# Z of batch 0 loaded in parts while its rows are made, in an FFT, channel mix and MLP kernel

## The chip, the cores and the metric

The kernel runs on one core of a Trainium2 chip. Its time is device microseconds of one launch. A median of several runs stands for a kernel; beside it there is one profiled execution, whose trace gives the rows that are shown here.

## What is computed

The input x has 8 batches of 3136 tokens and 256 channels, in float32. The first part goes through the frequency domain: a real FFT over the tokens, a complex channel mix, a soft threshold, and the inverse FFT. The second part adds a low-rank token mix and a two-layer MLP with a residual.

```python
X = np.fft.rfft(x, axis=1);  Xr, Xi = X.real, X.imag
Yr = Xr @ w_r - Xi @ w_i + b_r;  Yi = Xr @ w_i + Xi @ w_r + b_i
Y = soft(Yr, 0.01) + 1j * soft(Yi, 0.01)      # sign(v) * max(|v| - 0.01, 0)
y = np.fft.irfft(Y, n=3136, axis=1)
h = y.transpose(0, 2, 1) @ U @ V              # U is 3136 x 32, V is 32 x 3136
u = y + h.transpose(0, 2, 1)
out = u + np.maximum(u @ w_ch1, 0.0) @ w_ch2  # 256 -> 1024 -> 256
```

## The kernel before

The FFT of 3136 points is split into 49 x 64. For each batch there are four stages and then the MLP.

- Stage A makes products over the 49 points. Their rows go to the DRAM buffer gd. For batch 0 alone they stay in SBUF, in the tile t0.
- The frequency stage makes, for each pair of the frequencies 1 to 24 and for frequency 0 alone, the 64-point products (b_unit, PSUM psb), the channel mix (mix_unit, psy for batch 0), the soft threshold (rl on ScalarE, ys on VectorE), a split of the result into a high and a low part (yh on ScalarE, yl on GpSimd, which is written y where both stand in one tile), and the first half of the inverse (c_unit, psc). ScalarE evicts the result into a tile zs, and a DMA stores it as rows of the DRAM buffer zd. A pair with first frequency k0 writes the four rows from 2 k0 - 2 on; frequency 0 writes row 48. So zd has 49 rows of 64 tokens of 256 channels, 64 KB to a row.
- Stage D needs all 49 rows, turned: a tile zt holds, for 4 of the 32 token positions i and both halves j, the 49 rows on the partitions from 64 j on. It makes 512 small products of 49 x 64 by 49 x 81 in batch 0, four at a time in quarters of the array, into the PSUM tiles psd. ScalarE evicts them to xq, VectorE sums the part that belongs to U (pa). The right-hand sides du hold constants and U's part, which make_ud makes (psu).
- p_unit (psp, pt) and u_prep (psv) begin the MLP, whose token windows, six for each batch, follow one another. l1_chunks and l2_chunks are the layers (psx, psy, psz; pso), each a fast matrix product in split float32.

From window 0 on, the stages of the next batch run beside the MLP. Before window 0 only batch 0's stages can run, beside the decoding of the 64-bit weights: V, U, w1 and w2 come as words (dw) and are turned to float32 on ScalarE and VectorE, in tiles dm, dl, dp of the tag sv (four buffers). V's two halves go through a tile full of the tag tt (one buffer) to DRAM.

The order of the work has two sources. The function bodies record operations in a program order; for batch 0 a list called first holds units with a position, and is sorted: c_unit of unit q has position 3 q + 5, after_store(q) means 3 q + 5.5, and the units of D have 100, 105 and so on. The decoding is a generator that steps takes forward, a part at a time. Then a planner (class _Program, from line 166 on) sorts all operations by its own costs and due times, for each engine. All loads and stores but a few are issued by SyncE, in one queue; a load is released 16 us (LEAD) ahead of its due time. The buffers of a tag are given out in the order in which the program first touches them. Where the planner expects that TensorE will wait, it puts in matmuls of the identity (line 540, "ident"), as many as the expected gap divided by 0.222 us.

Frequency 0 is the last unit of batch 0 (pairs). Odd units put y and zs in the tag xz (five buffers), which the tiles zt of z use too; the last three zt stand in the tag rl. z_load (line 1085) is called by d_unit in D's place; for each c it issues two loads of 48 rows and one of row 48. Thus a load of z waits for a free buffer of xz or rl and for the stores of its rows. Loads of batch 1's input (xt, a_load, line 714) use the tag xz as well.

These lines say how z is loaded:

```python
pl, tg, n = (fp, "xz", 5) if b or c < 5 else (mp, "rl", 3)
zt = pl.tile([128, 4, D], F32, tag=tg, name=f"zt_{b}_{c}", bufs=n)
nk = KP if b else K1 - 1
loads = [dma.dma_start(zt[64 * j : 64 * j + nk], zv[c, j, 0:nk]) for j in range(2)]
if nk < K1:
    loads.append(dma.dma_start(by_row(zt)[nk], zv[c, :, nk]))
```

Of the kernel before, what the change touches and what calls it, by code (L numbers as in the profile page):

```python
# [13 lines left out]
F32 = mybir.dt.float32  # L14
# [536 lines left out]
def fft_mix_moe_kernel(  # L551
# [159 lines left out]
    def by_row(t):  # L711
        return t.rearrange("(j n) i d -> n j i d", j=2)

    def a_load(b, c):
        xt = fp.tile([128, 4, D], F32, tag="xz", name=f"xt_{b}_{c}", bufs=5)
        nk = KP if b < NB - 1 else K1 - 1
        n0, i = K1 * b, slice(4 * c, 4 * c + 4)
        loads = [dma.dma_start(xt[64 * j : 64 * j + nk], xj[n0 : n0 + nk, j, i]) for j in range(2)]
        if nk < K1:
            loads.append(dma.dma_start(by_row(xt)[nk], xj[n0 + nk, :, i]))  # L720
        a_state[b, c] = xt
        return loads

    def a_mm(b, c, loads=()):
# [51 lines left out]
    def shared(b):  # L776
        return b % 2 == 1 and b + 1 < NB

    def pairs(b):
        p = [(1 + 2 * q, 2) for q in range(12)]  # L780
        if shared(b):
            p.append((0, 2))
        elif b == 0 or b % 2 == 1:
            p.append((0, 1))
        return p

# [40 lines left out]
    def b_early(q):  # L827

        load_t(0, q)
        ts, fbt = s_state[0, q]  # L830
        ps = psm([128, 2, 2, 128], f"psb_0_{q}")
        for k in range(2):
            pe.matmul(ps[:, 0, k, :], lhsT=ts[k][0], rhs=fbt[:, k, :], start=True, stop=True)
        s_state[0, "ps", q] = ps

    def b_mm(b, q):
# [41 lines left out]
    def mix_unit0(q):  # L878
        n = pairs(0)[q][1]
        xx = s_state.pop((0, q, "x"))  # L880
        ps = ps_f.tile([128, 2, D], F32, tag="psf", name=f"psy_{q}")

        pe.matmul(
            ps[:, 0:n].rearrange("p k (n t) -> p k n t", t=2),
            lhsT=first_w["one"],
            rhs=paired(first_w["bias"]).unsqueeze(1).broadcast_to([128, n, D // 2, 2]),
            start=True,
            stop=False,
        )
        for k in range(n):  # L890
            todo = []
            for h in range(2):
                for c, w in ((1, wm[0]), (0, first_w["wi"])):
                    l = [x[:, h, k, c : c + 2].rearrange("p c f -> p (c f)") for x in xx]
                    todo.append((l, [v[:, h, :] for v in w]))
            for j, (l, w) in enumerate(todo):
                mm3(ps[:, k], l, w, False, k == n - 1 and j == len(todo) - 1, False)
        rl = ybuf(0, q, "rl")
        act.activation(rl[:, 0:n], ps[:, 0:n], AF.Relu, bias=lam)
        ys = ybuf(0, q, "ys")  # L900
        dve.scalar_tensor_tensor(
            out=ys[:, 0:n], in0=ps[:, 0:n], scalar=LAM, in1=rl[:, 0:n], op0=ALU.add, op1=ALU.min
        )
        if q % 2:
            both = fp.tile([128, 2, 2, D], F32R, tag="xz", name=f"y_0_{q}", bufs=5)
            yh, yl = both[:, 0], both[:, 1]
        else:
            yh, yl = [fp.tile([128, 2, D], F32R, tag="y" + k, name=f"y{k}_0_{q}", bufs=1) for k in "hl"]
        split(yh[:, 0:n], yl[:, 0:n], ys[:, 0:n], pool)
        s_state[0, q, "y"] = (yh, yl)  # L910

    def b_unit(b, q):
# [82 lines left out]
    def c_unit(b, q):  # L995
        k0, n = pairs(b)[q]
        yy = s_state.pop((b, q, "y"))
        pl, tg = (ps_f, "psf") if b or q % 2 == 0 else (ps_o, "pso1")
        ps = pl.tile([128, 2, D], F32, tag=tg, name=f"psc_{b}_{q}")
        mo = 128 if k0 else 64  # L1000
        mm3(ps[:mo, 0:n], fc if k0 else fc0, [k[:, 0:n] for k in yy], True, True, pairs=b > 0 or n == 2)
        if b == 0 and q % 2:
            zs = fp.tile([128, 2, D], F32, tag="xz", name=f"zs_{b}_{q}", bufs=5)
        else:
            zs = fp.tile([128, 2, D], F32, tag="zs", name=f"zs_{b}_{q}")
        if b == 0:
            zv = zs[:mo, 0:n].rearrange("p k (t n) -> p k t n", t=2)
            acopy(zv, flat(ps[:mo, 0:n]).rearrange("p (n t k) -> p k t n", k=n, t=2))
        elif n == 2:
            acopy(zs[:mo], halves(ps[:mo]))  # L1010
        else:
            acopy(whole2(zs[:mo, 0:1]), halves2(ps[:mo, 0:1]))
        if k0:
            dma.dma_start(rows(zd[b % 2], k0), zs)
        else:
            for k in range(n):
                dma.dma_start(zd[(b + k) % 2][K1 - 1], zs[0:64, k])
# [64 lines left out]
    def pad_z(k):  # L1082
        dma.dma_start(zd[k][K1:KP], x[0, 0 : (KP - K1) * N2].rearrange("(k n) d -> k n d", k=KP - K1))

    def z_load(b, c):

        pl, tg, n = (fp, "xz", 5) if b or c < 5 else (mp, "rl", 3)
        zt = pl.tile([128, 4, D], F32, tag=tg, name=f"zt_{b}_{c}", bufs=n)
        zv = zd[b % 2].rearrange("k (j c i) d -> c j k i d", j=2, i=4)
        s_state[b, "z", c] = zt  # L1090
        nk = KP if b else K1 - 1
        loads = [dma.dma_start(zt[64 * j : 64 * j + nk], zv[c, j, 0:nk]) for j in range(2)]
        if nk < K1:
            loads.append(dma.dma_start(by_row(zt)[nk], zv[c, :, nk]))
        return loads

    def dt_load(b, t):
        n0, n = UNITS_D[t]
# [6 lines left out]
    def d_unit(b, t, du, loads=()):  # L1105
        if t == 0:
            p_state[b] = qp.tile([128, 2, 3, R], F32, tag="pa", name=f"pa_{b}", bufs=1)
        n0, n = UNITS_D[t]
        hf = n0 // NH
        if n0 % NH == 0:  # L1110
            xq[b, hf] = qp.tile([128, 2, NH, NP], F32, tag="xq", name=f"xq_{b}_{hf}", bufs=3)
        if du is None:
            dt_ = s_state.pop((b, "d", t))
        else:
            dt_ = du[t]
            for c in range(8):
                if 4 * c < n0 + n and (b, "z", c) not in s_state:
                    z_load(b, c)
        pa = p_state[b]
        xv_ = xq[b, hf].rearrange("p h i (q j) -> p h j i q", j=2)  # L1120
        i0 = n0 % NH
        for h in range(2):
            turn_d[0] += 1
            ps = banks(turn_d[0] if b == 0 else 0, f"psd_{b}_{t}_{h}")

            def products():
                for k in range(n):
                    at = C81 * k - R * (k % 2)
                    for j in range(2):
                        for e in range(2):  # L1130
                            pe.matmul(
                                ps[j][64 * e : 64 * e + 64, at : at + C81],
                                lhsT=s_state[b, "z", (n0 + k) // 4][
                                    64 * j : 64 * j + K1,
                                    (n0 + k) % 4,
                                    128 * h + 64 * e : 128 * h + 64 * e + 64,
                                ],
                                rhs=dt_[64 * j : 64 * j + K1, C81 * k : C81 * k + C81],
                                start=k == 0,
                                stop=k == n - 1,  # L1140
                                tile_position=(64 * j, 64 * e),
                                skip_group_check=True,
                            )

            first = in_group(products)
            if h == 0:
                first.preds.update((e.n, e) for e in loads)
            for j in range(2):
                p = ps[j][:, 0 : n * C81]
                acopy(xv_[:, h, j, i0 : i0 + n], p.rearrange("p (n c) -> p n c", c=C81)[:, :, 0:K1])  # L1150
                u = p.rearrange("p (q c) -> p q c", c=2 * C81)[:, :, K1:C81]
                if t == 0 and j == 0:
                    dve.tensor_copy(pa[:, h], u)
                else:
                    v = pa[:, h, 0 : n // 2]
                    dve.tensor_tensor(out=v, in0=v, in1=u, op=ALU.add)
# [50 lines left out]
    def load_words(src, shape, name):  # L1207
        pp, *dims = shape
        n = int(_np.prod(dims))
        w = mp.tile([128, 1024], U32, tag="rh", name="dw_%s%d%d" % name, bufs=3)  # L1210
        w = w[:pp, : 2 * n].rearrange("p (n t) -> p n t", t=2)
        dma.dma_start(w if len(dims) == 1 else w.rearrange("p (f d) t -> p f d t", f=dims[0]), src)
        words[name] = w

    def decode(name, hi=None, lo=None, full=None):
# [282 lines left out]
            after_mix(q, 1.5 + k + (q == 0), steps, 1)  # L1498
    after_mix(12, 2.6, steps, STEPS_W)
    on(99.5, wait_2)  # L1500
    for n in range(16):
        on(100.5 + 2 * n, steps, 1)

# [455 lines left out]
```

## Time and profile before

| what | value |
|---|---|
| median of 3 runs | 1606.91 us (1606.64 to 1608.23) |
| profiled execution | 1603.72 us |
| its span | 1601.9 us |
| mean granted clock of TensorE | 0.995 |
| instructions | 37505 |
| VectorE busy | 1268.8 us (79%) |
| ScalarE busy | 937.5 us (59%) |
| GpSimd busy | 433.3 us (27%) |
| DMA | 209.16 MB, mean 131 GB/s |

The span runs from the first to the last instruction of the trace; the profiled execution's own time is 1.8 us longer. PE is TensorE, PEld its weight loads, DVE VectorE, ACT ScalarE, POOL GpSimd, SP SyncE. All operations go through one line of the planner, L542, so a row is told apart by the names of the tiles: psd<-du,zt is a product of stage D. L540 is a filler product. In a timeline a row gives the start, the duration, the operation, and in brackets the idle time of the engine before it with what ended it. In a table of windows the granted clock is 1.00 at full speed and 0.50 at half.

### The profile page before, as it was taken

What the parts mean: (1) busy time and instruction counts of PE and PEld (TensorE: products, weight loads), DVE (VectorE), ACT (ScalarE), POOL (GpSimd) and SP (SyncE); (2) the same over time, 40 slices, a digit from 0 to 9 for tenths busy, and PEclk for the clock granted to TensorE, in tenths of its full rate; (3) what the DMA queues carried; (4) which work ended last, traced back from release to release, by engine and by line L of the source; (5) the groups of instructions that cost most, each with busy time, mean ns of one, the idle gap of its engine ahead of it and who ended that gap; (6) DMA issues with size and microseconds to landing.
All of it is one profiled execution on the core that took longest, in us unless ns stands there. A gap on an engine that the chain in (4) does not pass through costs nothing.

```text
span 1601.9 us, 37505 instructions
## 1 busy us (share of the span) xinstructions
PE 1575.6 (98%) x14528; PEld 1428.1 (89%) x14528; DVE 1268.8 (79%) x2478; ACT 937.5 (59%) x1982; POOL 433.3 (27%) x406
## 2 busy tenths in 40 slices
PE   8988999999999999999999999999999999999998
PEld 6986898999889889999888988989988999989997
DVE  6866889679966898769975888868996789866785
ACT  3855666556655666556655666556665566555543
POOL 1320333123312332223331233314331233312221
PEclk9989999999999999999999999999999999999999
DMA  9776564516664454714574365433756024520332
GB/s 235 207 162 183 152 195 133 153 52 175 181 177 116 127 158 117 177 31 133 154 202 116 112 178 150 117 91 86 180 147 197 28 74 128 130 75 14 81 61 39
DMA packets 224814, 209.16 MB, mean 131 GB/s; under 512 B 127834, under 2 KB 195968, under 8 KB 224588
## 3 DMA queue, kind: packets, MB, share of 16 engines
q1 hardware_dynamic: 221998, 205.90, 48.1%
q8 instruction: 115, 1.88, 0.5%
q10 hardware_dynamic: 2638, 0.86, 0.3%
q14 instruction: 63, 0.52, 0.1%
HBM read 126.59 MB, written 81.81 MB: 130 GB/s over the span
## 4 chain that ended last, share of the span: by engine, by line
PE 89%; DVE 5%; DMA 2%; issue 1%; ACT 1%; SPq 1%; POOL 1%; DVEq 0%; POOLq 0%; ACTq 0%
PE pso L542 31%; PE psy L542 16%; PE psx L542 8%; PE psq L542 7%; PE psd L542 5%; PE psb L542 5%; PE psz L542 4%; PE psa L542 4%; PE psc L542 4%; PE pst L542 3%; PE psv L542 1%; SPq L542 1%; DVE ys L542 1%; DMA zd<-zs 1%; DVE s L542 0%
## 5 line engine op out<-in xcount | busy, mean ns | idle before, releaser
L542 PE MATMUL pso<-rh,w2t 128*128 128x512 f32 x1568 | 405.3, 381 | 0.0
L542 PEld LDWEIGHTS pso<-rh,w2t 128*128 128x128 f32 x1568 | 274.5, 190 | 26.7
L542 PE MATMUL pso<-rl,w2t 128*128 128x512 f32 x784 | 233.4, 379 | 0.0
L542 POOL TENSOR_TENSOR yl<-ys,yh 128x512 fp32r<-128x512 f32 (+1 forms) x95 | 122.5, 1290 | 219.8 <-ACT yh L542 121.2
L542 ACT ACTIVATE rh<-s 128x512 fp32r<-128x512 f32 x196 | 122.2, 628 | 89.6 <-DVE s L542 82.9
L542 DVE SCALAR_TENSOR_TENSOR rl<-s,rh 128x512 fp32r<-128x512 f32 x196 | 149.3, 767 | 25.2 <-ACT rh L542 23.6
L542 DVE SCALAR_TENSOR_TENSOR ys<-tb,rl 64x256 f32<-64x256 f32 x350 | 155.1, 443 | 16.7 <-ACT rl L542 12.0
L542 PEld LDWEIGHTS pso<-rl,w2t 128*128 128x128 f32 x784 | 148.3, 189 | 20.9
L542 POOL TENSOR_TENSOR tl<-ts,th 128x256 fp32r<-128x256 f32 x88 | 66.9, 760 | 300.3 <-DVE ys L542 130.4
L542 PE MATMUL psq<-wmt,xsh 128*128 128x256 f32 (+1 forms) x704 | 123.5, 277 | 0.0
L542 PE MATMUL psy<-odh,w1t 128*128 128x256 f32 x784 | 122.8, 279 | 0.0
L542 PEld LDWEIGHTS psy<-odh,w1t 128*128 128x128 f32 x784 | 109.8, 191 | 10.4 <-issue 2.4
L542 PEld LDWEIGHTS psq<-wmt,xsh 128*128 128x128 f32 (+1 forms) x704 | 109.3, 191 | 2.6 <-ACT xt L542 0.8
L542 POOL TENSOR_TENSOR obl<-xq,obh 128x512 fp32r<-128x512 f32 x47 | 58.7, 1249 | 194.5 <-ACT obh L542 51.4
L542 POOL TENSOR_TENSOR ocl<-xq,och 128x256 fp32r<-128x256 f32 x47 | 34.5, 733 | 244.3 <-DVE tt L542 92.9
L542 ACT ACTIVATE xq<-psd 128x294 f32<-128x294 f32 (+1 forms) x192 | 69.7, 437 | 50.0 <-PE psd L542 48.8
L542 DVE TENSOR_TENSOR v<-v,psy 128x512 f32<-128x512 f32 x98 | 66.7, 680 | 40.1 <-PE psy L542 21.6
L542 PE MATMUL psq<-wmt,xsl 128*128 128x256 f32 (+1 forms) x352 | 96.8, 275 | 0.0
L542 ACT ACTIVATE rh<-v 128x512 fp32r<-128x512 f32 x98 | 61.8, 631 | 59.4 <-DVE v L542 57.2
L542 DVE TENSOR_TENSOR s<-psz,s 128x512 f32<-128x512 f32 x98 | 67.2, 686 | 36.7 <-PE psz L542 27.4
L542 POOL TENSOR_TENSOR odl<-tt,odh 128x512 fp32r<-128x512 f32 x48 | 64.0, 1334 | 112.1 <-ACT odh L542 87.9
L542 PE MATMUL psb<-fb,t 128*128 128x128 f32 (+1 forms) x700 | 92.7, 276 | 0.0
(209 smaller groups left out, 3971.2 us busy)
## 6 DMA issues: line engine op xcount, KB each, us to landing
gd<-xt SPq DMA_DIRECT2D x112, 224.0 KB
zt<-zd SPq DMA_DIRECT2D x112, 224.0 KB
zd<-zs SPq DMA_DIRECT2D x96, 256.0 KB
out_dram<-os SPq DMA_DIRECT2D x190, 128.0 KB
xt<-in_x_dram SPq DMA_DIRECT2D x96, 224.0 KB
t<-gd SPq DMA_DIRECT2D x84, 256.0 KB
fb<-in_fb_dram SPq DMA_DIRECT2D x96, 128.0 KB
vw<-vd SPq DMA_DIRECT2D x44, 256.0 KB
```

Of the source, the lines that this page charges most:

```text
L542: made = call(*[real(a) for a in op.args], **{k: real(a) for k, a in op.kw.items()})
```

## The change

Frequency 0 becomes the first unit of batch 0. The odd units' zs move from the tag xz to the tag tt. The last two units (q 11 and 12) split y on VectorE instead of GpSimd. Stage D of batch 0 no longer calls z_load. Instead z is loaded into four tiles: two of 12 positions each in the tag xq (three buffers, of which fdt, the constants for make_ud, has one), one in the tag os, one in xz. Each tile gets its rows in three parts: rows 0 to 23 and row 48 after the stores of unit 6, rows 24 to 39 after those of unit 10, rows 40 to 47 at position 99.6. The loads of batch 1's input, all but those of the first tile, and the loads of words that come later in the program than the second part, wait for the latest part of z (after_z). Batches 1 to 7 load z as before.

```diff
     def a_load(b, c):
...
+        if b == 1 and c > 0:
+            for e in loads:
+                after_z(e)
...
     def pairs(b):
         p = [(1 + 2 * q, 2) for q in range(12)]
-        if shared(b):
+        if b == 0:
+            p.insert(0, (0, 1))
+        elif shared(b):
             p.append((0, 2))
-        elif b == 0 or b % 2 == 1:
+        elif b % 2 == 1:
             p.append((0, 1))
...
-        for k in range(2):
-            pe.matmul(ps[:, 0, k, :], lhsT=ts[k][0], rhs=fbt[:, k, :], start=True, stop=True)
+        k0, n = pairs(0)[q]
+        kk = 128 if k0 else 64
+        for k in range(n):
+            pe.matmul(ps[:, 0, k, :], lhsT=ts[k][0][:kk], rhs=fbt[:kk, k, :], start=True, stop=True)
...
-        split(yh[:, 0:n], yl[:, 0:n], ys[:, 0:n], pool)
+        split(yh[:, 0:n], yl[:, 0:n], ys[:, 0:n], pool if q < 11 else dve)
...
         if b == 0 and q % 2:
-            zs = fp.tile([128, 2, D], F32, tag="xz", name=f"zs_{b}_{q}", bufs=5)
+            zs = mp.tile([128, 2, D], F32, tag="tt", name=f"zs_{b}_{q}")
...
+    Z_CUT = (0, 24, 40, K1 - 1)
+    z_parts = ((0, 3), (3, 3), (6, 1), (7, 1))
+
+    def z_range(c, n, j, k0, k1):
+        zt = s_state[0, "zp", c]
+        src = zd[0][k0:k1, 32 * j + 4 * c : 32 * j + 4 * c + 4 * n]
+        return dma.dma_start(zt[64 * j + k0 : 64 * j + k1], src)
+
+    def z_early(m):
+        c, n = z_parts[m]
+        if n == 3:
+            zt = qp.tile([128, 12, D], F32, tag="xq", name=f"zx_{c}", bufs=3)
+        elif c == 6:
+            zt = mp.tile([128, 4, D], F32, tag="os", name="zt_0_6")
+        else:
+            zt = fp.tile([128, 4, D], F32, tag="xz", name="zt_0_7", bufs=5)
...
+        for j in range(2):
+            z_range(c, n, j, *Z_CUT[0:2])
+            z_range(c, n, j, K1 - 1, K1)
+
+    z_end = []
+
+    def z_late(m, part):
+        c, n = z_parts[m]
+        z_end[:] = [z_range(c, n, j, *Z_CUT[part : part + 2]) for j in range(2)]
+
+    def after_z(load):
+        load.preds.update((e.n, e) for e in z_end)
+        return load
...
-            for c in range(8):
-                if 4 * c < n0 + n and (b, "z", c) not in s_state:
-                    z_load(b, c)
...
-        dma.dma_start(w if len(dims) == 1 else w.rearrange("p (f d) t -> p f d t", f=dims[0]), src)
+        after_z(dma.dma_start(w if len(dims) == 1 else w.rearrange("p (f d) t -> p f d t", f=dims[0]), src))
...
+    for m in range(4):
+        after_store(6 + m / 2, z_early, m)
+        after_store(10 + m / 2, z_late, m, 1)
+        on(99.6, z_late, m, 2)
```

More of the change, by code (lines that the diff above doesn't have):

```diff
@@ L1083, in pad_z, with z_rows @@
         dma.dma_start(zd[k][K1:KP], x[0, 0 : (KP - K1) * N2].rearrange("(k n) d -> k n d", k=KP - K1))
+    def z_rows(b, c):
+        return zd[b % 2].rearrange("k (j c i) d -> c j k i d", j=2, i=4)[c]
     def z_load(b, c):
-        pl, tg, n = (fp, "xz", 5) if b or c < 5 else (mp, "rl", 3)
-        zt = pl.tile([128, 4, D], F32, tag=tg, name=f"zt_{b}_{c}", bufs=n)
-        zv = zd[b % 2].rearrange("k (j c i) d -> c j k i d", j=2, i=4)
+        zt = fp.tile([128, 4, D], F32, tag="xz", name=f"zt_{b}_{c}", bufs=5)
         s_state[b, "z", c] = zt
[L1091 to L1095, printed above, removed]
+        return [dma.dma_start(zt[64 * j : 64 * j + KP], z_rows(b, c)[j, 0:KP]) for j in range(2)]
+    Z_CUT = (0, 24, 40, K1 - 1)
[12 more added lines that the diff above has]
+            zt = fp.tile([128, 4, D], F32, tag="xz", name="zt_0_7", bufs=5)
+        s_state[0, "zp", c] = zt
+        for k in range(n):
+            s_state[0, "z", c + k] = zt[:, 4 * k : 4 * k + 4]
+        for j in range(2):
[8 more added lines that the diff above has]
+        return load
     def dt_load(b, t):
```

## The prediction

> **What bounds the kernel now.** I read the page first, then the table of ten-microsecond windows, then the chain of work that ended last, and then the timelines of single engines around the place that the chain points to.
>
> ```profile
> span 1601.9 us, 37505 instructions
> PE 1575.6 (98%) x14528; PEld 1428.1 (89%) x14528; DVE 1268.8 (79%) x2478; ACT 937.5 (59%) x1982; POOL 433.3 (27%) x406
> ```
>
> TensorE is busy for 98% of the span, so it has 26.3 us of idle time in all. A gain has to come from there, or from busy time that isn't work. The windows (width; busy us and instructions of PE, PEld, DVE, ACT and POOL; granted clock; DMA share; GB/s) show where that is:
>
> ```profile
> 100.00:110.00 10.00, 7.02 (x63) 6.83 (x62) 5.40 (x10) 1.31 (x2) 0.00 (x0) 1.00 1.01 172
> 110.00:120.00 10.00, 8.89 (x307) 8.73 (x307) 3.06 (x13) 4.79 (x15) 0.00 (x0) 0.66 0.74 211
> 120.00:130.00 10.00, 6.74 (x218) 6.49 (x219) 6.09 (x21) 4.55 (x14) 0.00 (x0) 0.88 0.76 188
> 220.00:240.00 20.00, 20.00 (x153) 19.19 (x152) 18.57 (x41) 14.46 (x36) 9.25 (x9) 1.00 0.50 155
> ```
>
> At 220 us TensorE has no gap. From 100 to 130 us it has 7.35 us of gaps, the DMA engines are full at first (share 1.01), and the clock falls to 0.66. A microsecond won ahead of the first MLP window is therefore a microsecond of the span. The chain (start, us, what) and TensorE's timeline (in brackets: idle time ahead, and who ended it) say what fills the stretch:
>
> ```profile
> 95.89 0.39 ACT zs L542
> 96.29 9.28 DMA zd<-zs
> 105.63 5.00 DMA zt<-zd
> 110.67 8.89 PE psd L542 x307
> 119.57 2.26 issue
> 121.83 2.49 PE psd L542 x124
> 124.31 1.43 issue
> 125.74 1.64 PE psd L542 x68
> 127.39 3.49 PE psp L540 x16
> ...
> 133.44 0.44 PE psa L540 x4
> ```
>
> ```profile
> 95.69 11.33 PE L540 MATMUL psd<-ident 128*128 128x128 f32 x100
> 110.67 8.89 PE L542 MATMUL psd<-du,zt 49*64 49x81 f32 x307 [3.66 <-DMA zt<-zd]
> ```
>
> The last row of z, frequency 0's, leaves its PSUM bank at 96.28 us. Its 64 KB store then takes 9.28 us, and the load of that row 5.00 us. TensorE runs 100 filler matmuls (line 540) of 11.33 us in that time and idles 3.66 us more. Then stage D needs 16.72 us (110.67 to 127.39), of which 2.26 + 1.43 = 3.69 us are waits. SyncE's queue shows why a 64 KB store is slow:
>
> ```profile
> 92.49 3.58 SPq L542 DMA_DIRECT2D zt<-zd  x8
> 97.09 10.97 SPq L542 DMA_DIRECT2D zt<-zd  x10
> 115.12 5.79 SPq L542 DMA_DIRECT2D xt<-in_x_dram  x8
> ```
>
> Eight loads of z of 192 KB each were issued just ahead of it. The waits inside D fall where the last loads of z and eight loads of batch 1 are under way together. The clock in D shows in windows of two microseconds (columns as above):
>
> ```profile
> 112.00:114.00 2.00, 2.00 (x70) 2.00 (x67) 0.51 (x2) 0.75 (x2) 0.00 (x0) 0.50 0.70 164
> 116.00:118.00 2.00, 2.00 (x88) 2.00 (x84) 0.56 (x3) 1.13 (x4) 0.00 (x0) 0.66 0.92 298
> 122.00:124.00 2.00, 2.00 (x120) 2.00 (x120) 0.67 (x2) 1.15 (x3) 0.00 (x0) 1.00 0.96 233
> ```
>
> At the half clock D makes 35 products in a microsecond, at the full clock 60. With 0.66 over 116 to 118 us, the half clock ended near 117.3 us: it held for some 6.6 us of D.
>
> **The change, term by term.** The sum is made against the profiled execution, 1603.72 us with a span of 1601.9; it lies 3.2 us below the median of the runs shown, 1606.91, so the difference is applied to the median.
>
> *First term, the end of the frequency stage.* Frequency 0 moves from the last place to the first, so the last store becomes a full pair's. The timelines of TensorE, ScalarE, GpSimd and VectorE give its steps:
>
> ```profile
> 78.33 0.28 PE L542 MATMUL psy<-wi,x3wm 128*128 128x256 f32 x1
> 89.52 0.38 PE L542 MATMUL psy<-b4r,one 128*128 128x256 f32 x1
> 90.74 0.58 PE L542 MATMUL psy<-wi,x3w 128*128 128x256 f32 x3
> 90.65 0.24 ACT L542 ACTIVATE x3w<-x3w 128x64 fp32r<-128x64 f32 x1
> 85.28 1.28 POOL L542 TENSOR_TENSOR y<-ys,y 128x512 fp32r<-128x512 f32 x1
> 129.64 0.69 DVE L542 TENSOR_TENSOR w2t<-dm,dp 128x512 fp32r<-128x512 f32 x1
> ```
>
> The evictions of the stage, as the view of the tile zs lists them (ns: least, median, most):
>
> ```profile
> L542 ACT ACTIVATE zs<-psc x15: 377/588/601, 40.2 to 193.8; 128x512 f32<-128x512 f32 x14, 64x256 f32<-64x256 f32 x1
> ```
>
> Before, the twelfth pair's mix ended at 78.6 us, but frequency 0's only at 91.3, as its last step on ScalarE came at 90.65, though nothing but other work of that engine was in its way. From there to its eviction at 96.28 went 4.97 us. A full pair's eviction is 0.21 us longer than frequency 0's (588 against 377 ns). Five such steps make 1.0 us more. The last split on VectorE instead of GpSimd (a 512-wide subtraction takes 0.69 there, 1.28 here) gives 0.6 back. So the latest end is 96.3 + 0.4 = 96.7 us, if the same weight work stays in the way. The earliest is reached if it is put behind. Then the mixes end at 78.6 plus frequency 0's own mix (89.52 to 91.32, 1.8 us), and with some 0.7 for its first products, an estimate, that is 81.1; the tail of 4.97 + 0.4 ends at 86.5. I take 93, nearer to the late end, since the weight decoding isn't removed and needs the same VectorE.
>
> *Second term, the store and the last loads.* The last part is eight rows: 512 KB in eight loads, after the landing of the last store of 256 KB. For quiet transfers the nearest rows of the chain are these:
>
> ```profile
> 17.25 4.14 DMA wis<-in_w_i_dram
> 61.44 1.71 DMA vd<-vh
> ```
>
> A 256 KB load landed in 4.14 us, with another of its size just ahead; a 64 KB store in 1.71. The ends are 1.71 + 1.71 = 3.4 and the 9.28 + 5.00 = 14.3 of before. I take 4.1 for each step, 8.2 us, the row with the nearest size: rows 0 to 23 with row 48, and rows 24 to 39, were asked for before, and batch 1's loads (all but two) wait for the last of z. Stage D needs only the first two loads (192 KB) to begin; the others land while it works. D then begins at 93 + 8.2 = 101.2 instead of 110.67: 9.5 us earlier.
>
> How many engines share those eight-row loads can't be read here. The Trainium skill (DMA: Bandwidth & Descriptors, why a DMA increments its semaphore by 16) says that a transfer runs on the largest number of engines, up to 16, that divides the slowest dimension of its patterns, which speaks against cutting off eight rows: eight engines. Against the 298 GB/s of the row at 116 us that would be 149, so 192 KB need 1.3 us instead of 0.65, and D would begin 0.65 us later. No row of before has such a load.
>
> *Third term, the length of D.* Its 512 products took 16.72 us; without the waits of 3.69 it is 13.0. I expect the waits to go, as the loads no longer share with batch 1's. The clock probably falls again, since the fillers are counted by the planner and in before ran out 3.66 us early. Half clock for 6.6 us gives 231 products. The other 281 at the pace of the end of D (192 in 2.49 + 1.64 us, 21.5 ns each) take 6.0. Together 12.6 us, 4.1 less than before. The ends are 512 x 16.7 ns = 8.5 and 16.7. ScalarE's evictions set another floor,
>
> ```profile
> 112.61 0.75 ACT L542 ACTIVATE xq<-psd 128x294 f32<-128x294 f32 x2 [8.86 <-PE psd L542]
> ```
>
> twelve such pairs of 0.75, 9.0 us. By the rows the clock comes back 6.6 us after the work does. The Trainium skill (TensorE: Matmul & The Clock Gate, the HAM clock gate) has it return after a busy window of about 3.4 us. By that rule, 119 products cold and 393 at 21.5 ns, D would take 11.8 us, 0.8 less. The trace of before doesn't agree: it took twice that.
>
> *Fourth term, D's end to window 0.* From 127.39 to the first product of batch 1's stage A at 133.44 are 6.05 us. Sixteen fillers of 3.49 us in it ran at 0.22 us each, twice the 0.113 of the hundred above; at the full clock 1.7 us would go. I count nothing.
>
> *Fifth term, what is given back.* The weights still have to be decoded.
>
> ```profile
> 36.19 0.53 DVE L542 TENSOR_TENSOR full<-dm_v,dp_v 128x392 f32<-128x392 f32 x1
> 45.85 4.10 SPq L542 DMA_DIRECT2D zd<-zs  x2
> 94.54 1.23 DVE L542 TENSOR_TENSOR w1t<-wa,w1t 128x512 fp32r<-128x512 f32 x1
> 104.98 0.69 DVE L542 TENSOR_TENSOR w2t<-dm,dp 128x512 fp32r<-128x512 f32 x1
> ```
>
> VectorE ended w1 at 95.8, three quarters of w2 at 105.7 and the last at 130.3 (row above). Between 100 and 130 us it was busy 14.55 of 30 us, so 15.4 us were free, and 13.6 us of that stretch are now cut. The odd pairs' zs also move into the single buffer tt, which V's decoding uses too. In program order pair 1's zs comes between V's two halves, so the second half (36.19 before) has to wait until pair 1's rows have landed: its store is issued at 45.85 or shortly after, so some 12 to 14 us. Behind it in the four sv buffers stand U's and w1's decodings. I give back 2.6 us, with ends of 0 and 8 (half of the 15.4). The longer waits of SyncE (z's loads for the stores of their rows, batch 1's and w2's loads for z) have fb and the stores of the next pairs queued behind them; three fb are loaded ahead, and I count this within the same ends. The two other edits (frequency 0's first product on 64 rows, z's buffers xq and os) cost nothing beside TensorE work that is there anyway; the buffers are empty until D, and batch 0's xq halves get fdt's and z's own slots as these are used up.
>
> The sum: 9.5 + 4.1 + 0 - 2.6 = 11.0 us, 0.7%. The median would be 1606.91 - 11.0 = 1595.9, say **1596 us**.
>
> **The rivals.** *The waiting only changes its name.* The planner releases a load 16 us ahead of its due time at most, so the early parts may be late and stand with the last one in the same full DMA. Then D begins at 96.7 + 14.3 = 111.0 as before, and only its inner waits go: 3.7 - 0.3, less the 2.6 given back, 0.8 us faster, 1606, which is no difference. For it: the DMA share of 1.01 from 100 us on. Against it: only 512 KB instead of some 3 MB are left by then. *The tail moves up.* If the weight work is put behind the last pair, the stage ends at 86.5, D begins at 94.7 and, with the full clock, takes 512 x 21.5 ns = 11.0 us; window 0 begins 22 us earlier, less up to 8 given back: 14 to 22 us faster, 1585 to 1593. For it: twelve mixes were done at 78.6. Against it: VectorE and GpSimd take turns up to 96 us, and have no less to do. *Slower: V's decoding behind pair 1's zs.* If the 14 us by which V's second half waits go through U and w1 into the end of the frequency stage, it ends at 96.3 + 14 = 110, D begins at 118.5, and window 0 begins 118.5 - 110.67 - 4.1 = 3.7 us later than before; with the 2.6 of the fifth term that is 6.3 us slower, 1613. It decides once more than 7.7 us of the 14 reach the last pair (96.3 + 7.7 + 8.2 + 12.6 + 2.6 = 127.4). For it: VectorE was busy almost without a gap up to 105 us. Against it: nothing of the pairs needs V, U or w1, and window 0 needs w1 only at 133 us.
>
> **How the numbers follow.** A measurement of this kernel can tell about 0.2%, 3.2 us, from no change. My forecast (4 to 14 us faster) has 0.60, the early tail 0.18, the wait that changes its name 0.12, slower 0.10. So faster by over 0.2% is 0.78, within 0.2% 0.12, slower 0.10. The range for 8 in 10 runs from 1586, nearly all of the early tail, to 1606, the end where D begins as late as before.
>
> **What the profile after would show.** If I am right, the chain's store and load of z are together near 8 us, D begins near 101 us without gaps longer than 1 us inside, the clock is at half speed for its first 3 to 7 us, batch 1's loads are issued behind z's, and the first psa starts near 120 us. V's second full on VectorE stands near 48 us instead of 36. From there to the end the distance is that of before, 1468 us to within 2. Wrong I would be with a store to zd still above 6 us at the end of the stage, with ScalarE waiting for tt at an odd pair's eviction, with the last eviction after 100 us, or with TensorE waiting for w1t or w2t in window 0.

## The result

| kernel | median of its runs | profiled execution, span |
|---|---|---|
| before | 1607.49 us (1606.64 to 1608.23, 4 runs) | 1603.72, 1601.9 |
| after | 1616.01 us (1615.66 to 1618.18, 4 runs) | 1616.18, 1614.4 |

The ratio is 1.0057, with a 95% interval of 1.0045 to 1.007: the change makes the kernel 9 us slower, where 11 us faster were forecast, and the time lies outside the range. First the page of after, then its table of windows (columns as before):

```profile
span 1614.4 us, 37399 instructions
PE 1582.6 (98%) x14486; PEld 1424.8 (88%) x14486; DVE 1268.9 (79%) x2480; ACT 937.9 (58%) x1982; POOL 429.4 (27%) x404
```

```profile
100.00:110.00 10.00, 6.91 (x205) 6.58 (x207) 2.15 (x7) 2.20 (x6) 1.26 (x1) 0.83 0.70 149
110.00:120.00 10.00, 5.02 (x226) 4.69 (x220) 4.10 (x16) 4.30 (x13) 0.00 (x0) 0.80 0.89 287
120.00:130.00 10.00, 9.34 (x169) 8.88 (x161) 7.56 (x20) 5.84 (x15) 0.00 (x0) 0.85 0.19 52
130.00:140.00 10.00, 9.15 (x35) 2.43 (x34) 7.55 (x14) 3.88 (x8) 0.00 (x0) 0.66 0.53 163
```

More products are done by 110 us (205 against 63), and then TensorE stands for half of the next ten. The chain of after says with what:

```profile
91.17 0.61 ACT zs L542
91.80 0.36 SPq L542
...
95.48 7.93 DMA zx<-zd
103.42 0.04 issue
103.46 0.36 PE psd L542 x4
103.82 1.24 issue
105.06 5.90 PE psd L542 x223
110.95 0.73 issue
111.68 2.49 PE psd L542 x126
114.17 4.26 issue
118.43 4.46 PE psd L542 x91
```

The frequency stage ends 4.5 us earlier (91.77 against 96.28), D begins 7.2 us earlier (103.46 against 110.67), but then it needs 20.13 us instead of 16.71 (16.72 by the chain), with 6.23 us in which TensorE waits for nothing that the profile names ("issue"). Window 0's first psa comes at 129.98 instead of 133.81. So 3.8 us of the lead are left at 130 us, and at its end after is 12.5 us behind (8.5 by the medians; the profiled execution of before was a quick one). The two stretches from 130 us to the end, in the tables of TensorE's windows, first of before and then of after (width; busy us and instructions; clock; DMA share; GB/s):

```profile
130.00:1601.90 1471.90, 1459.18 (x13205) 1.00 0.46 124
```

```profile
130.00:1614.40 1484.40, 1468.71 (x13179) 0.99 0.46 124
```

For nearly the same work TensorE is counted busy 9.5 us longer there and idle 3.0 us longer, though the change touches nothing behind window 0. What it does touch is the planner: its due times come from the whole program, so with another front all of the 1470 us behind it are put in another order. Part of the 9.5 us is the clock: in window 0 TensorE is busy without a gap for 10.2 us, but at the half clock, where before had the full clock (columns as in the first table, after above, before below):

```profile
133.20:143.40 10.20, 10.20 (x35) 4.37 (x34) 7.49 (x14) 4.21 (x9) 0.00 (x0) 0.50 0.65 192
```

```profile
131.10:145.00 13.90, 13.21 (x93) 8.60 (x92) 10.96 (x23) 6.51 (x14) 0.00 (x0) 1.00 0.53 166
```

By these rows the half clock cost at most 5.1 us there.

SyncE's queue in after, for the second term:

```profile
87.41 4.75 SPq L542 DMA_DIRECT2D zd<-zs  x2
92.25 1.80 SPq L542 DMA_DIRECT2D zx<-zd  x4
...
95.48 4.14 SPq L542 DMA_DIRECT2D zx<-zd  x4
100.69 3.01 SPq L542 DMA_DIRECT2D zt<-zd  x5
...
106.39 1.57 SPq L542 DMA_DIRECT2D dw<-in_moe_w_ch_dram  x2
108.06 1.26 SPq L542 DMA_DIRECT2D xt<-in_x_dram  x3
```

Rows 24 to 39 were to be loaded while the last pairs are made; they are issued at 92.25, behind the last two stores, at which SyncE had stood for 4.75 us. And batch 1's loads, held behind z, now start at 106 to 112 us, in the middle of D.

### The profile page after: what moved, and what is told of

It is laid out like the page before. It is cut to its first block, busy times and chain, and to the rows that moved or that the text cites. A ratio compares the mean times of both kernels' runs of the same rounds, so it can differ in the third digit from the quotient of the medians.

```text
span 1614.4 us, 37399 instructions
## 1 busy us (share of the span) xinstructions
PE 1582.6 (98%) x14486; PEld 1424.8 (88%) x14486; DVE 1268.9 (79%) x2480; ACT 937.9 (58%) x1982; POOL 429.4 (27%) x404
## 3 DMA queue, kind: packets, MB, share of 16 engines
q8 instruction: 115, 1.88, 0.5%
## 4 chain that ended last, share of the span: by engine, by line
PE 85%; DVE 8%; ACT 2%; issue 2%; DMA 2%; SPq 0%; POOL 0%; DVEq 0%; ACTq 0%; POOLq 0%
PE pso L542 29%; PE psy L542 16%; PE psx L542 8%; PE psq L542 6%; PE psd L542 6%; PE psb L542 5%; PE psa L542 5%; PE psz L542 4%; PE psc L542 3%; PE pst L542 3%; DVE ys L542 2%; PE psv L542 1%; DVE rl L542 1%; DVE tb L542 1%; DVE s L542 1%
## 5 line engine op out<-in xcount | busy, mean ns | idle before, releaser
L542 ACT ACTIVATE yh<-ys 128x512 fp32r<-128x512 f32 (+1 forms) x95 | 59.6, 627 | 53.3 <-DVE ys L542 48.8
```

The costliest lines, as they stand in the source:

```text
L542: made = call(*[real(a) for a in op.args], **{k: real(a) for k, a in op.kw.items()})
```

## The experiments

Two theories. A: the front of the change is worth little either way, and the loss comes from the new order of all later work. B: the front itself sets the loss off. Each ratio below is to the kernel before in runs on the same chip, with its 95% interval. The code cuts are shortened: names such as in_front, name(o) or depends_on_held stand for several lines.

**The order alone.** The planner was run for both programs. The front then follows one plan, and everything that a plan starts behind 260 us the other.

```diff
+    key[o.n] = (0, oa.start, o.n) if in_front or ob.start <= 260.0 else (1, ob.start, o.n)
+    order = sorted(a.ops, key=lambda o: key[o.n])
```

> The kernel after up to the planner's time 260 us (the front and what runs beside it), and behind that every instruction in the order in which the kernel before has it. Theory A (the front of the change is worth little either way, and some 10 us are lost because the planner, given other due times, orders all later windows anew): the time falls from 1616.0 to about 1609, at most 3 us over the kernel before, and TensorE's idle time after 130 us falls from 21.3 us to within 4 us of the 10.8 of before. Theory B (the front itself sets off the loss: decoding that comes late, weights late, a clock that falls in window 0): the time stays at 1614 to 1618 and the idle time with it.

> The reverse: the kernel before up to the planner's time 260 us, and behind that the order of the kernel after. Theory A: the loss is there without the change's front, 1614 to 1618 us, though z is loaded as before. Theory B: within 3 us of the kernel before, 1605 to 1610.

For the other two, the kernel before was planned again with slightly shifted due times (the numbers are the seed, the standard deviation of the shift in us, and the first and last due time that is shifted):

```diff
-CHANGES = ()
+CHANGES = ((1, 0.5, 300.0, 1e9),)    # second run: (2, 0.5, 300.0, 1e9)
```

> The kernel before, in which every due time behind 300 us of the plan is shifted by a random number of 0.5 us standard deviation, and the planner then orders the work; up to there nothing differs. Theory A says that the order of later work alone moves the time by several us: 1602 to 1620, with differences of idle time in windows that the change does not touch. Theory B has no use for such scatter: within 3 us of the kernel before.

> As the run before it, with other random numbers. Theory A: again some other time between 1602 and 1620, not that of the first by more than chance. Theory B: within 3 us of the kernel before.

| kernel | median | ratio |
|---|---|---|
| front after, rest before | 1605.67 us | 0.9997 (0.9988 to 1.0006) |
| front before, rest after | 1613.12 us | 1.0040 (1.0025 to 1.0055) |
| before, replanned, first | 1611.30 us | 1.0030 (1.0018 to 1.0041) |
| before, replanned, second | 1613.54 us | 1.0049 (1.0032 to 1.0065) |

Theory A holds in all four. The front of the change with the old order behind it costs nothing and gains nothing; the new order costs 0.4%, 6.4 us, without the front; and two orders that differ from the old one only by chance cost 5 and 8 us. Theory B's numbers are missed each time, A's 1614 to 1618 for the second by 1 us. The idle time, on which A was to be seen too, shows nothing: the 21.3 and 10.8 us in that text were summed over stretches of unequal length; from 130 us to each span's end it is 15.7 us in after, 12.7 in before (the rows above) and 15.0 in the first of these kernels. So the order costs more than TensorE's plain waiting. Nor is it the clock alone: the mean granted clock over all runs of a kernel is 0.9935 for before and 0.9932, 0.9925, 0.9928 and 0.9940 for the four of the table, so the slowest of them has the highest clock. The chain fits better, though not sharply. The engines' shares in the chains of before, of the first and of the second kernel are these:

```profile
PE 89%; DVE 5%; DMA 2%; issue 1%; ACT 1%; SPq 1%; POOL 1%; DVEq 0%; POOLq 0%; ACTq 0%
```

```profile
PE 90%; DVE 4%; DMA 2%; issue 2%; ACT 1%; SPq 1%; POOL 0%; DVEq 0%; ACTq 0%; POOLq 0%
```

```profile
PE 81%; DVE 9%; ACT 2%; issue 2%; DMA 1%; POOL 0%; SPq 0%; DVEq 0%; POOLq 0%; ACTq 0%
```

With the other orders (this one, the two replanned, after itself) VectorE carries 7 to 9% of the chain. With the old order it was 2 to 7%. The two ranges touch, and two of the chains with the old order (V's halves elsewhere and the best kernel below) reach back over only half of the span, so what makes an order slow stays open. One reading was not tried: the planner's constants may have been set so that this one order came out well, and then almost any other would be slower.

**What lengthens D.** The front should have brought more than nothing. The next run empties D's surroundings.

```diff
+    gate = dma_start(scr, xq[0, 1][0:64, 1, NH - 1])     # reads D's last eviction
+    held = [o for o in order[last_z_load + 1 : end_of_D + 1] if o.eng == "sp" or depends_on_held(o)]
+    order = [o for o in order[: end_of_D + 1] if o not in held] + [gate] + held + order[end_of_D + 1 :]
```

> The first of these experiments (the front of after, the rest in the order of before), with every transfer and decoding that was issued between the last load of z and the end of D held until D's last eviction, by a small store that reads it. So nothing but the last loads of z moves while D's products run; window 0 comes later for it, and the time with it, which is not asked here. In the kernel without this hold D's products stood still three times for no semaphore, 1.08, 3.63 and 1.12 us together 5.83. Theory F (PE's instructions are loaded by the same DMA engines, and the bulk loads of batch 1 that the change puts right into D delay that): these stretches fall under 2 us in sum, and D takes 12 to 14 us from its first product to its last. Theory G (D's short products use instructions up faster than they can be loaded, whatever else is moved): 3.5 to 6 us of such stretches stay, and D takes 17 to 20 us.

Its time, 1609.38 us in one run, is not the point here. The window of D, from its first product to its last, in the first experiment and in this one (columns as in the tables of windows):

```profile
104.42:124.70 20.28, 14.45 (x513) 13.74 (x513) 8.08 (x28) 9.02 (x25) 0.00 (x0) 0.73 0.73 198
```

```profile
103.42:118.61 15.19, 11.86 (x513) 11.24 (x513) 5.33 (x22) 7.62 (x22) 0.00 (x0) 0.89 0.14 21
```

With 21 GB/s beside it instead of 198, D takes 15.19 us. The waits fall from 5.83 to 3.33 us, the longest of them from 3.63 to 1.44, and the clock is less often halved. F names the right cause, but its 2 us and 12 to 14 us were too good; something of G remains. (A like hold further down gave 15.24 us with the same front, and 14.64 with V's halves moved besides, so the quiet D does not rest on one execution.) What TensorE waits for can be seen in the page of after and in the DMA queues of its D (packets, MB, share):

```profile
q8 instruction: 115, 1.88, 0.5%
```

```profile
q8 instruction: 4, 0.07, 1.5%
```

1.88 MB for 14486 products and 14486 weight loads are 65 bytes each, so queue q8 most likely loads TensorE's instructions, 16 KB or some 250 of them at a time. D's 512 products and 512 weight loads need four such loads. The trace's list of transfers has them start 3.8 to 4.0 us apart in the quiet D, and up to 6.1 us apart in the first experiment. Four times 3.9 is 15.6 us, about the quiet D's whole length. So D's products seem to be so short that the loading of instructions sets their pace, and bulk transfers beside it slow that down. The trace has no event that says so, but the times agree closely: all "issue" waits that the eighteen timelines list inside D, 34 of them, end 2.2 to 3.2 us after such a piece began to move. In after they end at 111.68 and 118.43, behind pieces at 109.20 and 115.95; in the quiet D at 113.89 and 117.82, behind 111.27 and 115.20. Not counted in this is the wait right behind D's first four products in the kernels that load z in the change's way (1.24 us in after, 1.08 and 1.21 in the two windows above): it ends over 4 us behind a piece, and where the profile names a releaser for it, in five of these ten kernels, that is DMA zx<-zd. So it is most likely a load of z. Without it the waits for instructions fall from 4.75 to 2.12 us, near F's 2.

This is no matter of how z is loaded. The D of before, of the second experiment, and of the replanned ones has the same order of instructions in all four:

```profile
110.67:127.38 16.71, 13.02 (x513) 12.60 (x513) 6.84 (x26) 8.29 (x25) 0.00 (x0) 0.80 0.78 205
```

```profile
112.58:132.01 19.43, 14.11 (x513) 13.61 (x513) 7.32 (x27) 8.43 (x24) 0.00 (x0) 0.76 0.72 196
```

The other two are 20.25 and 16.07 us. So one order gives 16.1 to 20.3 us, and the change's front gave 20.1 to 21.5 in four executions (after, the first experiment, and the two with a part moved that follow). The 3.4 us by which D grew from before to after need not all be the change's; what the change did not bring is the D without waits that was forecast.

**Parts of the front.** Three runs, on the first experiment or on before:

```diff
+    order = moved(order, part_1_loads, behind=store_of_unit_10)     # ahead of the last two stores
```

> The first of these experiments with one move on SP's queue: the eight loads of part 1 (rows 24 to 39) stand ahead of the two last stores and not behind them. If SP's order is what brings the last loads of z late (16 loads issued behind 93.4 us, landing one after the other), the first product of D begins at 99 to 101.5 us and not at 104.4, and the total falls by 0 to 3 us against the experiment without the move, less than D's start gains, if D's own waits grow again. The rival, that the last part alone sets D's start, gives 104 to 105 us again and the same total.

```diff
-        full = mp.tile([128, 392], F32, tag="tt", name=f"full_{c}")
+        full = fp.tile([128, 4, D], F32, tag="xz", name=f"full_{c}", bufs=5)
```

> The first of these experiments with the two halves of V in the buffers of x and z instead of those that the change gives to odd zs tiles; the front is planned anew with it, the rest keeps the order of before. V's second half is then written some 10 us earlier (near 36 us and not 47). If the late V is what costs the front 2 us on TensorE near 30 us and the late decoding behind it, D's start and window 0 come 1 to 3 us earlier and the total falls by as much. If V lies off the path, the total stays within 1 us, 1604 to 1607.

```diff
-        elif b == 0 or b % 2 == 1:
+        elif b % 2 == 1:                                      # and p.insert(0, (0, 1)) for b == 0
```

> The kernel before with frequency 0 first in batch 0 and nothing else of the change: z is loaded in one piece behind the last store, and batch 1's loads are not held; the front is planned anew, the rest keeps the order of before. I expect 1 to 2 us more at 30 us, where there is less work in the first pair, and 1605 to 1610 us in all. If frequency 0 first were itself a gain, the last store would be issued 3 us or more ahead of the 94 us or so of before, and the total 1600 to 1604.

The loads of part 1 moved ahead gave 1606.27 us, 1.0002 (0.9992 to 1.0012), with D's first product at 104.29: the rival was right. SyncE's queue there:

```profile
88.21 1.72 SPq L542 DMA_DIRECT2D zx<-zd  x4
89.97 1.81 SPq L542 DMA_DIRECT2D zt<-zd  x4
...
93.55 1.92 SPq L542 DMA_DIRECT2D zd<-zs  x2
100.83 1.30 SPq L542 DMA_DIRECT2D zx<-zd  x4
```

The last pair's products now ended earlier (89.47 against 91.36), but the last two stores stood behind eight loads and the last part was issued only at 100.83. Putting part 1 first only moves the same transfers in front of the stores. V's halves elsewhere (the second at 31.63 us) gave 1605.60 us, 0.9988 (0.9979 to 0.9998): some 2 us by the ratio, and 1.4 against the first experiment's 0.9997, with intervals that overlap. Frequency 0 first alone gave 1608.66 us, 1.0017 (1.0008 to 1.0027), as expected slightly slower; D, with fillers inside it, took 21.58 us. This kernel also keeps the change's split of the last two units on VectorE, so it is not quite frequency 0 alone.

**The loads held behind D for good.** If bulk loads beside D cost some 5 us, holding them should pay. The gate now reads D's fifth unit, x goes ahead of the words, and the decoding of the held words goes behind pt. The second run has V's halves elsewhere besides, the third is the kernel before with this hold alone.

```diff
-    gate = dma_start(scr, xq[0, 1][0:64, 1, NH - 1])
+    gate = dma_start(scr, xq[0, 1][0:64, 1, NH - 5])
+    loads.sort(key=lambda o: not name(o).startswith(("xt", "fq")))
+    order = order[: end + 1] + [gate] + loads + order[end + 1 : pt + 1] + decoding + order[pt + 1 :]
```

> The first of these experiments (front of after, rest in the order of before), with batch 1's loads of x, the words of w2 and the stores of du held behind the eviction of D's fifth unit of six, x ahead of the words, and the decoding of those words behind the products with pt. Theory F (bulk loads beside D delay the loading of PE's instructions): D takes 15 to 16.5 us from its first product to its last, as in the quiet D (15.1) and not 20.2, and window 0's first psa comes at 126 to 128.5 us and not at 131.5. The total then falls by 0 to 4 us against the first experiment, to 1602 to 1606, less than window 0 gains if the words of w2 come late. The rival, that the loads held back are needed at once in window 0, gives psa at 130 us or later and no gain in all.

> The run before it, with the two halves of V in the buffers of x and z besides (the front planned anew). If the two gains add up, D begins at 102 us, window 0's first psa comes at 124 to 127 us, and the total is 1600 to 1605. If they do not, it is that of the run before it to within 2 us.

> The kernel before, with nothing of the change, and batch 1's loads of x, two loads of words and the stores of du that stand behind its last load of z held behind the eviction of D's fifth unit. Theory F: D, which took 16.7 us with stretches of 2.26 and 1.43 us without a semaphore, takes 14 to 15.5 us here too, so that these stretches are no matter of how z is loaded. Theory G (the loading of instructions is too slow for D whatever moves): 16 us or more again. In all 1603 to 1609, since x of batch 1 now comes later to window 0.

All three were slower: 1613.62 us, 1.0052 (1.0035 to 1.0069); 1612.57 us, 1.0040 (1.0025 to 1.0055); 1615.29 us, 1.0060 (1.0045 to 1.0075). The gains that were expected, to between 1600 and 1609 us, did not come. D did what was expected (15.24, 14.64 and 13.52 us; this is the window of the third, the kernel before):

```profile
111.88:125.40 13.52, 12.51 (x513) 12.08 (x513) 4.86 (x21) 7.37 (x22) 0.00 (x0) 0.79 0.14 39
```

and window 0 lost all of it. TensorE's second psa product and ScalarE in the first of the three:

```profile
139.03 2.57 PE L542 MATMUL psa<-xt,fq 49*64 49x512 f32 x8 [10.62 <-DVE xq L542]
```

```profile
129.25 0.66 ACT L542 ACTIVATE dm<-dw 128x512 f32<-128x512 f32 x1 [5.66 <-DMA dw<-in_moe_w_ch_dram]
```

The words came at 129 us, their decoding stood in VectorE's queue ahead of xq's sum, and that sum ahead of window 0. In all three the clock fell too, by the traces' clock records to one half for 17 to 20 us in a stretch (131.2 to 148.3 us in the first). So x, du and fq alone were held next, and the words left where they were:

```diff
-    loads = [o for o in order[begin : last + 1] if o.eng == "sp"]
+    loads = [o for o in order[begin : last + 1] if o.eng == "sp" and name(o).startswith(("xt", "dud"))] + [fq_load]
```

> V's halves in the buffers of x and z, front of after, rest in the order of before; of what moved beside D only batch 1's loads of x, the stores of du and fq are held behind the eviction of D's fifth unit (fq first); the words of w2 and their decoding stay where they stood, so that nothing stands in VectorE's way in window 0. If the loss of the runs with all of it held came from that decoding, D still takes under 17 us, window 0's first psa comes at 124 to 127 us and the second within 2.5 us of it, and the total falls to 1600 to 1604. If x itself is needed as early as it came, window 0 waits for its loads and the total is 1605 or more.

> The same hold without the move of V (the first experiment with the hold): D begins at 104 to 105 us and takes under 17 us, first psa at 127 to 129 us, total 1602 to 1606; or, if x is needed as early as it came, 1606 or more.

> The kernel before with the same hold and nothing of the change: D takes 13.5 to 15 us as it did with all held, window 0's first psa comes at 129 to 132 us, and without the decoding in VectorE's way the total comes back from 1615 to 1603 to 1608. If x alone is the reason (all of its first loads are held here), it stays above 1610.

1604.00 us, 0.9987 (0.9977 to 0.9996); 1604.92 us, 0.9994 (0.9984 to 1.0003); 1610.22 us, 1.0026 (1.0017 to 1.0036). D took 17.88, 16.89 and 13.89 us, the first above the 17 expected: three loads of words of 512 KB still ran beside it. It was the words and their decoding, for the most part: with the change's front the loss is gone, in the kernel before more than half of it, though its 1610.22 still lies above the 1610 that was given for x alone. There and in the first of the three ScalarE showed the next wait, in these rows:

```profile
138.15 0.26 ACT L542 ACTIVATE vr<-vraw 128x64 fp32r<-128x64 f32 x1 [11.64 <-DMA vraw<-vfl]
```

```profile
128.52 0.26 ACT L542 ACTIVATE vr<-vraw 128x64 fp32r<-128x64 f32 x1 [5.20 <-DMA vraw<-vfl]
```

vraw is four loads of 8 KB, issued behind the held ones. They were moved ahead of the gate:

```diff
+    words = [o for o in order[begin:] if o.eng == "sp" and name(o).startswith("vraw")][:4]
+    order = order[:begin] + words + [o for o in order[begin:] if o not in words]
```

> The run with x, du and fq held and V's halves moved, in which ScalarE stood 5.20 us for vraw, a small load that came behind the held ones, with window 0's conversions queued behind it. Here the four loads of vraw stand ahead of the hold. If that wait was on the path, the third psa product follows the second within 1 us (2.2 us of waiting before), window 0 gains 2 to 5 us, and the total is 1599 to 1603 against some 1606 of the kernel before. If x, whose loads now come behind D, ends next, the gain in window 0 is under 1 us and the total 1603 to 1606.

> The kernel before with x, du and fq held behind D's fifth unit, where ScalarE stood 11.64 us for vraw: here vraw's loads stand ahead of the hold. If that wait alone made it 0.26% slower, the total falls by 4 to 6 us to 1603 to 1606, at or under the kernel before. If x comes too late for window 0 by itself, it stays at 1608 or above.

The first gives 1600.19 us, 0.9968 (0.9956 to 0.9980): about 5 us faster than the kernel before, the best kernel of this study. The second gives 1608.44 us, 1.0018 (1.0006 to 1.0029). So vraw was worth about 3 us in the first and about 1 in the second; both are differences of ratios from different chips, with intervals that overlap. In the kernel before the hold still doesn't pay, and its time lies on the side that was given for x coming too late by itself. Its D ends 7.6 us later than that of the best kernel (126.91 against 119.35), and what is held comes later by as much; in its window 0 TensorE waits for vw, which SyncE issues behind x:

```profile
142.91 0.77 PE L542 MATMUL psv<-vw,pt 128*128 128x512 f32 x1 [3.99 <-DMA vw<-vd]
```

Whether that wait is all was not tried. With the change's front there is room for the hold, so the parted loading of z does bring something, once the order behind it is kept and the queues ahead of window 0 are set right. In the best kernel window 0's first psa stands at 126.85:

```profile
126.85 1.09 PE L542 MATMUL psa<-xt,fq 49*64 49x512 f32 x8
128.17 1.68 PE L542 MATMUL psa<-xt,fq 49*64 49x512 f32 x8 [0.23 <-DVE xq L542]
```

That kernel keeps the order of before behind 260 us. How it would do with the order that the planner makes of it was not tried.

## Why the prediction was wrong

**The step that failed** is the sentence that from window 0 to the end the distance is that of before, 1468 us to within 2. It was 1484.4. None of the rivals held this case, since all of them stopped at window 0. The new order costs 0.60% with the change's front (1.0057 against 0.9997, 9.6 us) and 0.40% with the old one (6.4 us). That is about half of the miss; the other half is the front, which with the old order behind it gave nothing (0.9997) where 11 us were forecast, and the second and third terms below say where they went. Not all of the 9.6 us need be the order as such: the mean granted clock was 0.991 over the four runs of after and 0.993 over the ten of the first experiment, which over 1614 us is 3 to 4 us, and in the profiled execution the half clock in window 0 is a part of it. Whether the order brought that about isn't shown. The description of the kernel named the planner; that it would plan the 1470 us behind the change anew should have been a rival with its own price, and that price could have been bounded only by replanning, as the two shifted runs did.

**A second fault may lie in the distance itself,** but it is not shown. In the profiles with the old order behind, and with nothing held or with vraw ahead, the distance from the first psa to the end is 1466.9 us (first psa at 139.94, frequency 0 first), 1468.1 (133.81, before) and 1473.2 to 1475.3 in the five others (131.71 to 126.85). It looks as if an early window 0 had a longer way to the end. But each is one execution, and executions of one kernel differ by several us: that of the best kernel took 1604.62 us, against its median of 1600.19. Over the 13.1 us between the first and the best kernel the spans fall by 4.7 us, the ratios to before by 7.9. So how much of a lead at window 0 reaches the end can't be read from these. Part of the longer distances is again the clock: by the trace's clock record the half clock lasts 5.2 to 5.4 us behind the first psa in the two with the short distances, 8.1 in the first experiment, and 13.2 to 14.5 in the other four, and half of that difference, up to 4.6 us, is the most that it can cost.

First term: 93 expected, 91.77 measured, right (92.93 in the first experiment, with the same front).

Second term: 8.2 us expected, 11.7 measured (91.77 to 103.46). The store is no longer on the chain; in its place stand 3.7 us in which SyncE issues it and part 1 (91.80 to 95.48), and then 7.93 us instead of 4.1 for the loads. I had part 1 out of the way by then. The four loads of 96 KB, 8 rows each, took SyncE 4.14 us to issue (the row at 95.48), the four of 192 KB ahead of them 1.80, since by their spacing, 1.5 us, each had to wait until an earlier load had landed. The name-changing rival described this in part. On the eight rows: no run isolates how many engines such a load has, so what the Trainium skill (DMA: Bandwidth & Descriptors, why a DMA increments its semaphore by 16) says stays untested here.

Third term: 12.6 us expected, 20.13 measured. The waits inside D were put down to the loads of z sharing with batch 1's. But their rows said "issue" and named no DMA, unlike the 3.66 us ahead of D's first product: no semaphore was waited for. By the runs with D kept quiet, and by the times of queue q8, they are most likely the loading of TensorE's own instructions, which bulk transfers slow; in after these waits are 4.99 of the 6.23 us. The same edit that I took as their cure, batch 1's loads held behind z, puts those loads beside D. A pace of 21.5 ns for each product, on which 6.0 us of the sum rest, was not kept over a whole D in any run: the shortest, with 39 GB/s beside it, took 13.52 us, 26 ns each, with 5.7 us at the half clock by the trace's clock record. The clock was halved twice, once behind the stops around D's start and once in the longest wait. These windows of after hold its two returns:

```profile
108.00:110.00 2.00, 2.00 (x89) 0.69 0.93 331
...
122.00:124.00 2.00, 2.00 (x65) 0.77 0.04 8
```

0.69 and 0.77 over two microseconds put the end of the half clock at 109.2 and 122.9, 4.2 and 4.5 us after the products went on (105.06, 118.43). My 6.6 was too long for after. The Trainium skill (TensorE: Matmul & The Clock Gate, the HAM clock gate) with about 3.4 us was nearer. In the trace's clock record the two stretches at the half clock last 3.41 and 6.83 us, and the one around D of before 6.83.

Fourth term: 6.05 us expected, 6.24 measured to the same point, the filler ahead of the first psa (133.44 is such a filler and not, as the term has it, a product of stage A); to the first real psa it is 6.43 before and 6.39 after. Right. Fifth term: V's second full stands at 46.81 us, 10.6 us later than before, where some 12 to 14 were forecast:

```profile
46.81 0.56 DVE L542 TENSOR_TENSOR full<-dm_v,dp_v 128x392 f32<-128x392 f32 x1
```

Its price was about 2 us by the run that moved it, within the 2.6 given back. The slower rival, V's delay running through to the last pair, didn't happen: the last pair ended early. The kernel was slower for a reason that this rival did not have.

## What to carry to other kernels

Where a planner orders the whole program, an edit in the first tenth reorders the other nine; freeze the order behind the edit, and replan the old kernel a few times with shifted due times, before a difference of half a per cent is put down to the edit. A wait without a semaphore in a stage of many short instructions can be the loading of the instructions: look at the bytes that move beside it, and keep bulk transfers out of that stage. Whoever holds a load back holds back all that is queued behind its consumer: first the decoding on VectorE, then a small load that ScalarE needed. With all of it held, the kernels lost more in window 0 than D had won.

## What the runs showed of the hardware

- Queue q8 moves 16 KB pieces whose sum is 65 bytes for each TensorE instruction; 34 waits for no semaphore in D ended 2.2 to 3.2 us after such a piece began to move. The pieces started 3.4 to 4.0 us apart at best in D. D, 512 products and 512 weight loads in four pieces, took 13.5 to 15.2 us with 21 to 39 GB/s beside it; with 74 to 112 GB/s D took 13.9 to 17.9 us, with 185 to 215 it took 16.1 to 21.6.
- The half clock of TensorE comes in whole multiples of 3.41 us in the traces' clock records, apart from the stretch that the end of the execution cuts: 3.41, 6.83, 10.24, 17.07 and 20.48 us.
- One order of instructions in D, up to the planner's 260 us, gave lengths from 16.07 to 20.25 us in one execution each of four kernels. A single profile's stage is not known better than to 4 us here.
- The later work, put in two other orders that differ from the old one only by chance, was 5 and 8 us slower than the old one. Why the old one is better than these was not settled.
